# A fourth block product split into seven small ones in the channel product of an attention and mixer kernel

## The chip, the core and the metric

The kernel runs on one core of one Trainium2 chip. The metric is the device time of one execution in microseconds; the kernel before takes 827.31 us (median of three runs, 827.25 to 828.09). The core's engines work side by side and wait for each other by semaphores: TensorE (PE) multiplies matrices into the PSUM buffer, and its weight loads are listed as PEld; VectorE (DVE) and ScalarE (ACT) read PSUM and work on SBUF. Every tensor that the change touches is float32.

## The reference

Routed attention gives `x`, and a mixer follows it. The change lies in the mixer's first channel product, `u @ w_ch1`, and in the relu behind it.

```python
def _moe_ref(x, w_tok1, w_tok2, w_ch1, w_ch2):        # x: (4, 768, 512), from the attention
    xt = x.transpose(0, 2, 1)
    h = np.maximum(xt @ w_tok1, 0.0) @ w_tok2
    u = x + h.transpose(0, 2, 1)
    h2 = np.maximum(u @ w_ch1, 0.0) @ w_ch2           # w_ch1: (512, 1536), w_ch2: (1536, 512)
    return (u + h2).astype(np.float32)
```

## The kernel before

The first channel product is computed transposed, `h2.T = w_ch1.T @ u.T`, as a product of two-by-two blocks with **seven** block products in place of eight (Winograd's form of Strassen's method). The sums of the left blocks (`S1`, `S2`, `S3`, `S4`) are made from weights, those of the right blocks (`T1` to `T4`) from the activations. The table says for each product its PSUM tag, its left and right factor, and the output block to which the running sum in its bank is added when it is done.

```python
SEVEN = {
    "p1":  ("X", "A11", "B11", "c11"),
    "p5":  ("Z", "S1",  "T1",  "c22"),
    "c11": ("Y", "A12", "B21", "c11"),
    "u2":  ("X", "S2",  "T2",  "c12"),    # accumulated on p1, in the same bank
    "c12": ("Z", "S4",  "B22", "c12"),
    "c22": ("X", "S3",  "T3",  "c22"),    # accumulated on p1 + u2
    "c21": ("X", "A22", "T4",  "c21"),
}
```

The rows of the output are worked off in three parts for each of four batches, twelve calls of `ch1_pair` in all. In each call a block product has two chunks (`i`) of 128 rows by 384 columns, and contracts over 256 (`k`), so it takes four matmuls of 384 columns:

```python
def product(psum, a, r, i, start):                    # line 797 of the profile
    c = slice((part + 3 * i) * P, (part + 3 * i + 1) * P)
    for k in range(2):
        nc.tensor.matmul(psum, lhsT=A[a][:, k, c], rhs=R[r][:, k],
                         start=start and k == 0, stop=k == 1, ...)
```

In the first call all seven products are made so. In the other eleven ("with sets") three of them, Y (`c11`), Z (`c12`) and X (`c21`), are themselves two-by-two block products made of seven **small** products, of one matmul of 192 columns each. After every small product the running sum in its bank is added to the output by VectorE, and only then may the next one be accumulated onto that bank:

```python
def set_(psum, which, name, start):                   # line 810 of the profile
    _, a, r, _ = SEVEN[name]
    nc.tensor.matmul(psum, lhsT=left[which][a][:, part * P : part * P + P],
                     rhs=right[which][r], start=start, stop=True, ...)

def set_x(which, tag, name, x):
    if tag: chains[which] = ptile(tag, HS // 2)
    bank = chains[which]
    set_(bank, which, name, name == "p1")
    add(x, both(bank) if len(x.shape) == 3 else bank, x)
```

The head of `ch1_pair` with sets (HS is 384, `n0` and `n1` are the two halves of 192 columns; `between()` works off waiting pieces of other work, such as sums for later; `big` is `product` and then `between()`):

```python
for i in range(2):
    X[i] = ptile("X", HS); big(X[i], "A11", "B11", i, True)
    nc.scalar.copy(out=a11[:, i], in_=X[i])
Z[0] = ptile("Z", HS); big(Z[0], "S1", "T1", 0, True)          # p5, four matmuls over both chunks
nc.scalar.copy(out=p5[:, 0], in_=Z[0])
yc = ptile("X", HS)
set_(yc[:, n0], "Y", "c11", True); set_(yc[:, n1], "Y", "c12", True)
add(a11[:, 0], yc, a11[:, 0])
set_x("Y", "Y", "p1", a11[:, 0, n0])
Z[1] = ptile("Z", HS); big(Z[1], "S1", "T1", 1, True)
nc.scalar.copy(out=p5[:, 1], in_=Z[1])
set_x("Y", None, "u2", a11[:, 0, n1])
set_z("Y", ptile("Y", HS // 2), a11)
big(X[0], "S2", "T2", 0, False); nc.scalar.copy(out=u2[:, 0], in_=X[0])
# ... cut: the second chunk, the rest of Y, Z accumulated on the banks Z[0] and Z[1] ...
relu(a11)                                                      # one instruction, 768 elements
# ... cut: S3 T3, the rest of Z ...
relu(a22)
set_x("Z", None, "c22", c12[:, 1]...)
set_(X[0][:, n0], "X", "c11", False); set_(X[0][:, n1], "X", "c12", False)
nc.scalar.copy(out=a12[:, 0], in_=X[0])
set_(X[1][:, n0], "X", "c21", False)
nc.scalar.copy(out=a12[:, 1], in_=X[1])
set_x("X", "Y", "p1", a12[:, 0, n0]); sum_1()
# ... cut: three more small products of X run inside the second channel product ...
```

Behind each `ch1_pair` follows `ch2_chunks` (line 953 of the profile): the second channel product, 21 chunks of two matmuls of 256 columns, with a VectorE sum into `x` after each. PSUM has eight banks here: three of tag X, three of tag Z and two of tag Y. Between two batches the next batch's activations are turned (`u_steps`) and their right sums made (`u_sums` for the seven products, `set_right_sums` for the small ones).

Of the kernel before, what the change touches and what calls it, by code (L numbers as in the profile page):

```python
# [50 lines left out]
def kernel(  # L51
# [497 lines left out]

    SEVEN = {  # L550
# [16 lines left out]
    def left_weights():  # L567

        w = W["ch1"]
        half = DCH // 2  # L570
        A = pools["A"] = {
            f"A{i + 1}{j + 1}": w[:, 2 * j : 2 * j + 2, half * i : half * i + half]
            for i in range(2)
            for j in range(2)
        }
        extra = pools["wsums"].tile([P, 3, 2, half], F32, name="w1s")
        A["S1"], A["S2"], A["S4"] = (extra[:, i] for i in range(3))
        A["S3"] = A["A21"]
# [22 lines left out]
    def set_lefts():  # L601
        if "l2" not in pools:
            pools["l2"] = pools["w2sums"].tile([P, 3, 3, HS], F32, name="w1ss")
        A, l2 = pools["A"], pools["l2"]
        both = W["ch1"].rearrange("p f (i r c) -> p f i r c", i=2, r=2)[:, 2:4]
        single = A["S4"].rearrange("p f (r c) -> p f r c", r=2)
        for blocks, sums_ in (
            ([both[:, f, :, r] for r in range(2) for f in range(2)], [l2[:, 0:2, m] for m in range(3)]),
            ([single[:, f, r] for r in range(2) for f in range(2)], [l2[:, 2, m] for m in range(3)]),
        ):  # L610
# [9 lines left out]
    def set_rights():  # L620
        uT, t4, r2 = pools["uT"], pools["R"]["T4"], pools["r2"]
        both = uT[:, :, 2:4].rearrange("p n f (k t) -> p n f k t", k=2)
        single = t4.rearrange("p f (k t) -> p f k t", k=2)
        for blocks, sums_ in (
            ([both[:, :, f, k] for f in range(2) for k in range(2)], [r2[:, 0:2, m] for m in range(3)]),
            ([single[:, f, k] for f in range(2) for k in range(2)], [r2[:, 2, m] for m in range(3)]),
        ):
            yield dict(
                zip(("B11", "B12", "B21", "B22", "T1", "T2", "T4", "T3"), blocks + sums_ + blocks[1:2])
            )  # L630

    def set_right_sums():
        pools["r2"] = pools["w2sums"].tile([P, 3, 3, HS // 2], F32, name="uTss")
        for blocks in set_rights():
            yield from winograd_right(blocks)

    def set_blocks():

        (yx, z), (yz, x) = (list(y) for y in (set_lefts(), set_rights()))
        left = {"Y": {k: a[:, 0] for k, a in yx.items()}, "X": {k: a[:, 1] for k, a in yx.items()}, "Z": z}  # L640
        right = {"Y": {k: b[:, 0] for k, b in yz.items()}, "Z": {k: b[:, 1] for k, b in yz.items()}, "X": x}
# [139 lines left out]
    def ch1_pair(part, sets, beside):  # L781
# [6 lines left out]
        p5, u2, c12 = (pools["mlp"].tile([P, 2, HS], F32, name=k) for k in ("p5", "u2", "c12"))  # L788
        A, R = pools["A"], pools["R"]
        left, right = set_blocks() if sets else (None, None)  # L790
        n0, n1 = slice(0, HS // 2), slice(HS // 2, HS)
        X, Y, Z, chains = {}, {}, {}, {}
# [15 lines left out]
        def set_(psum, which, name, start):  # L808
# [6 lines left out]
        def both(psum):  # L815
            return psum.unsqueeze(1).to_broadcast([P, 2, HS // 2])

        def relu(x):
            nc.scalar.activation(out=x, in_=x, func=ACT.Relu)  # L819


        def set_x(which, tag, name, x):
            if tag:
                chains[which] = ptile(tag, HS // 2)
            bank = chains[which]
            set_(bank, which, name, name == "p1")
            add(x, both(bank) if len(x.shape) == 3 else bank, x)

        def set_z(which, bank, x):
            set_(bank, which, "p5", True)  # L830
            add(x[:, :, n1], both(bank), x[:, :, n1])

        a11, a12, a22 = h2["A11"], h2["A12"], h2["A22"]
        for i in range(2):
            X[i] = ptile("X", HS)
            big(X[i], "A11", "B11", i, True)
            nc.scalar.copy(out=a11[:, i], in_=X[i])  # L837
        Z[0] = ptile("Z", HS)
        big(Z[0], "S1", "T1", 0, True)
        nc.scalar.copy(out=p5[:, 0], in_=Z[0])  # L840
        if sets:
            yc = ptile("X", HS)
            set_(yc[:, n0], "Y", "c11", True)
            set_(yc[:, n1], "Y", "c12", True)
            add(a11[:, 0], yc, a11[:, 0])
            set_x("Y", "Y", "p1", a11[:, 0, n0])
        Z[1] = ptile("Z", HS)
        big(Z[1], "S1", "T1", 1, True)
        nc.scalar.copy(out=p5[:, 1], in_=Z[1])
        if sets:  # L850
            set_x("Y", None, "u2", a11[:, 0, n1])
            set_z("Y", ptile("Y", HS // 2), a11)
        else:
            Y[0] = ptile("Y", HS)
            big(Y[0], "A12", "B21", 0, True)
            add(a11[:, 0], Y[0], a11[:, 0])
        big(X[0], "S2", "T2", 0, False)
        nc.scalar.copy(out=u2[:, 0], in_=X[0])
        if sets:
            set_x("Y", None, "c22", a11[:, 1, n1])  # L860
            set_(Z[0][:, n0], "Z", "c11", False)
            set_(Z[0][:, n1], "Z", "c12", False)
        else:
            Y[1] = ptile("Y", HS)
            big(Y[1], "A12", "B21", 1, True)
            add(a11[:, 1], Y[1], a11[:, 1])
        big(X[1], "S2", "T2", 1, False)
        nc.scalar.copy(out=u2[:, 1], in_=X[1])
        if sets:
            set_x("Y", None, "c21", a11[:, 1, n0])  # L870
            relu(a11)
            set_(Z[1][:, n0], "Z", "c21", False)
            add(c12[:, 0], Z[0], u2[:, 0])
            set_x("Z", "Z", "p1", c12[:, 0, n0])
            add(c12[:, 1], Z[1], u2[:, 1])
        else:
            relu(a11)
            big(Z[0], "S4", "B22", 0, False)
            add(c12[:, 0], Z[0], u2[:, 0])
        big(X[0], "S3", "T3", 0, False)  # L880
        add(a22[:, 0], X[0], p5[:, 0])
        if sets:
            set_x("Z", None, "u2", c12[:, 0, n1])
            set_z("Z", ptile("Y", HS // 2), c12)
        else:
            big(Z[1], "S4", "B22", 1, False)
            add(c12[:, 1], Z[1], u2[:, 1])
        big(X[1], "S3", "T3", 1, False)
        add(a22[:, 1], X[1], p5[:, 1])
        relu(a22)  # L890
        if sets:
            set_x("Z", None, "c22", c12[:, 1].rearrange("p (k t) -> p k t", k=2))
            set_(X[0][:, n0], "X", "c11", False)
            set_(X[0][:, n1], "X", "c12", False)
            nc.scalar.copy(out=a12[:, 0], in_=X[0])  # L895
            set_(X[1][:, n0], "X", "c21", False)
            nc.scalar.copy(out=a12[:, 1], in_=X[1])


        def sum_3():  # L900
            nc.vector.scalar_tensor_tensor(
                out=h2["S3"], in0=c12, scalar=0.0, in1=a11, op0=ALU.max, op1=ALU.subtract
            )

        def sum_1():
            nc.vector.scalar_tensor_tensor(
                out=h2["S1"], in0=c12, scalar=0.0, in1=a22, op0=ALU.max, op1=ALU.add
            )

        def sum_4():  # L910
            sub(h2["S4"], a12, h2["S2"])

        if sets:
            set_x("X", "Y", "p1", a12[:, 0, n0])
            sum_1()

            def late_1():
                set_x("X", None, "u2", a12[:, 0, n1])
                set_z("X", ptile("Z", HS // 2), a12)
                sub(h2["S2"], h2["S1"], a11)  # L920

            def late_2():
                set_x("X", None, "c22", a12[:, 1].rearrange("p (k t) -> p k t", k=2))
                relu(a12)
                sum_3()
                sum_4()

            late.extend([late_1, late_2])
        else:
            sum_1()  # L930

            def late_(i):
                product(X[i], "A22", "T4", i, False)
                nc.scalar.activation(out=a12[:, i], in_=X[i], func=ACT.Relu)
                if i == 0:
                    sub(h2["S2"], h2["S1"], a11)
                else:
                    sum_3()
                    sum_4()

            late_(0)
            late.append(lambda: late_(1))
# [210 lines left out]
    for n, b in enumerate(batches):  # L1153
        turning = []
        for part in range(3):
# [9 lines left out]
            if first:  # L1165
                others += list(set_right_sums()) + list(right_weights(1))
# [8 lines left out]
            if part == 2 and not last:  # L1175
                after[3] = lambda: take(turning, len(turning))
                after[15] = lambda: next(usums)
                usums = u_sums()
            ch2_chunks(b, part, last, after)
# [3 lines left out]
            if part == 2 and not last:  # L1183

                steps = list(set_right_sums())
                for m in range(2):
                    steps[m]()
                next(usums)
# [221 lines left out]
```

## Time and profile before

| what | value |
|---|---|
| median time | 827.31 us |
| span of the profiled execution | 825.8 us, granted clock 1.000 |
| busy PE, PEld | 818.2 us (99%), 525.9 us (64%) |
| busy DVE, ACT, POOL | 605.1 us (73%), 381.5 us (46%), 30.7 us (4%) |
| instructions of PE, DVE, ACT | 4282, 1124, 562 |
| the chain that ended last | PE 95%, DVE 4% |

"Busy" is the time in which at least one instruction of the engine ran. A matmul of float32 stands in the trace as two records. Matmuls overlap in the pipeline, and the ends of their records are modelled; so the durations of records are longer than the distance from one start to the next, and it is the starts that tell how fast TensorE goes on. In a line of instruction groups stand the program line, engine, operation, output and input tiles, shapes, count, then busy time and mean duration, and last the idle time before them with what ended it. In a timeline, a line begins with the start and the length in microseconds, and ends, where the engine was idle before, with the idle time and its releaser. A table by stage gives for each stretch its length, then busy time and number of instructions of each engine.

### The profile page before, as it was taken

What the parts mean: (1) busy time and instruction counts of PE and PEld (TensorE: products, weight loads), DVE (VectorE), ACT (ScalarE), POOL (GpSimd) and SP (SyncE); (2) the same over time, 40 slices, a digit from 0 to 9 for tenths busy, and PEclk for the clock granted to TensorE, in tenths of its full rate; (3) what the DMA queues carried; (4) which work ended last, traced back from release to release, by engine and by line L of the source; (5) the groups of instructions that cost most, each with busy time, mean ns of one, the idle gap of its engine ahead of it and who ended that gap; (6) DMA issues with size and microseconds to landing.
All of it is one profiled execution on the core that took longest, in us unless ns stands there. A gap on an engine that the chain in (4) does not pass through costs nothing.

```text
span 825.8 us, 11453 instructions
## 1 busy us (share of the span) xinstructions
PE 818.2 (99%) x4282; PEld 525.9 (64%) x4282; DVE 605.1 (73%) x1124; ACT 381.5 (46%) x562; POOL 30.7 (4%) x28
## 2 busy tenths in 40 slices
PE   8999999999999999999999999999999999999997
PEld 4444444444444444444588787878878788787876
DVE  6879898989898968859776677655667466764645
ACT  5588777787878775136202253121441204521120
POOL 1001010111111000000000000000000000000000
PEclk9999999999999999999999999999999999999999
DMA  8697666767676334143000125000140001400002
GB/s 152 142 159 144 135 142 121 152 143 159 136 156 144 84 96 121 51 156 48 0 1 1 20 39 173 1 0 7 36 113 1 1 1 29 126 1 0 1 2 79
DMA packets 184256, 63.39 MB, mean 77 GB/s; under 512 B 172800, under 2 KB 176896, under 8 KB 183936
## 3 DMA queue, kind: packets, MB, share of 16 engines
q1 hardware_dynamic: 182592, 62.18, 34.5%
q8 instruction: 35, 0.57, 0.3%
q10 hardware_dynamic: 1600, 0.39, 0.2%
q14 instruction: 29, 0.24, 0.1%
HBM read 36.21 MB, written 7.86 MB: 53 GB/s over the span
## 4 chain that ended last, share of the span: by engine, by line
PE 95%; DVE 4%; ACT 0%; issue 0%; ACTq 0%; DVEq 0%
PE sc L413 19%; PE av L455 15%; PE pX L953 14%; PE pX L797 11%; PE pZ L953 7%; PE ph L534 5%; PE pY L810 4%; PE pY L953 4%; PE pZ L797 3%; PE pZ L810 3%; PE pX L771 3%; PE pX L810 2%; PE small L491 2%; PE pZ L771 1%; PE small L304 1%; DVE hA L565 1%
## 5 line engine op out<-in xcount | busy, mean ns | idle before, releaser
L437 ACT ACTIVATE ex<-sc 128x768 f32<-128x768 f32 x192 | 151.0, 812 | 27.2 <-PE sc L413 15.5
L413 PE MATMUL sc<-qkT 64*128 64x384 f32 x768 | 155.3, 483 | 0.0
L445 DVE TENSOR_TENSOR sum<-sum,ex 128x768 f32<-128x768 f32 x128 | 127.8, 998 | 27.6 <-ACT ex L437 15.5
L455 PE MATMUL av<-ex,va 128*64 128x384 f32 x768 | 127.4, 488 | 0.0
L565 DVE TENSOR_TENSOR x<-pX,x 128x256 f32<-128x256 f32 (+1 forms) x168 | 75.9, 458 | 40.9 <-PE pX L953 40.4
L455 PEld LDWEIGHTS av<-ex,va 128*64 128x64 f32 x768 | 53.7, 137 | 71.8 <-issue 67.0
L413 PEld LDWEIGHTS sc<-qkT 64*128 64x128 f32 x768 | 67.8, 187 | 38.3 <-issue 38.0
L837 ACT COPY hA<-pX 128x384 f32<-128x384 f32 x24 | 11.5, 479 | 146.0 <-PE pX L797 146.0
L565 DVE TENSOR_TENSOR hA<-pY,hA 128x192 f32<-128x192 f32 (+1 forms) x90 | 36.7, 408 | 49.9 <-PE pY L810 36.0
L819 ACT ACTIVATE hA<-hA 128x768 f32<-128x768 f32 x35 | 29.5, 843 | 87.1 <-DVE hA L565 87.1
L797 PE MATMUL pX<-uT,wc 128*128 128x384 f32 x192 | 68.0, 487 | 0.0
L413 PE MATMUL sc<-ohT 64*128 64x384 bf16 x384 | 62.5, 323 | 0.0
L797 PEld LDWEIGHTS pX<-uT,wc 128*128 128x128 f32 x192 | 35.7, 190 | 17.6 <-issue 0.6
L462 ACT COPY avrows<-av 128x768 uint16<-128x768 uint16 x32 | 25.5, 798 | 43.9 <-PE av L455 43.9
L565 DVE TENSOR_TENSOR x<-pZ,x 128x256 f32<-128x256 f32 (+1 forms) x84 | 36.4, 455 | 12.0 <-PE pZ L953 11.9
L534 PE MATMUL ph<-x,wt 128*128 128x512 f32 x96 | 41.6, 593 | 0.0
L413 PEld LDWEIGHTS <-ohT 64*128 64x128 bf16 x384 | 18.7, 94 | 33.8 <-issue 9.6
L953 PE MATMUL pX<-wc,hA 128*128 128x256 f32 x144 | 36.9, 380 | 0.4 <-ACT hA L895 0.4
L708 ACT COPY uT<-ucols 128x768 uint16<-128x768 uint16 x32 | 33.3, 1051 | 4.5 <-DMA ucols<-urows 4.5
L953 PE MATMUL pY<-wc,hA 128*128 128x256 f32 x144 | 35.1, 379 | 0.0
L953 PE MATMUL pZ<-wc,hS 128*128 128x256 f32 x144 | 35.0, 379 | 0.0
L797 PE MATMUL pX<-uTs,w1s 128*128 128x384 f32 x96 | 34.9, 486 | 0.0
(178 smaller groups left out, 1266.0 us busy)
## 6 DMA issues: line engine op xcount, KB each, us to landing
raw<-in_moe_w_ch_dram SPq DMA_DIRECT2D x24, 512.0 KB, 4.5
va<-in_v_dram SPq DMA_DIRECT2D x16, 384.0 KB, 3.6
out_dram<-x SPq DMA_DIRECT2D x24, 256.0 KB, 2.5
qk<-in_k_dram SPq DMA_DIRECT2D x60, 96.0 KB, 3.8
qk<-in_q_dram SPq DMA_DIRECT2D x60, 96.0 KB, 3.5
raw<-in_moe_w_tok_dram SPq DMA_DIRECT2D x3, 512.0 KB, 4.2
raw<-in_moe_w_tok_dram SPq DMA_DIRECT2D x4, 384.0 KB, 3.9
spill<-x SPq DMA_DIRECT2D x1, 1536.0 KB, 5.1
```

Of the source, the lines that this page charges most:

```text
L413: nc.tensor.matmul(sc[:, h, 0:HS], lhsT=src[rows, 1, j], rhs=src[rows, 0, HJ * qh : HJ * qh + HJ], start=start, stop=not start,)
L437: nc.scalar.activation(out=ex, in_=sc[:, :, 0:HS], func=ACT.Exp, scale=SM_SCALE)
L445: nc.vector.tensor_tensor(out=acc, in0=acc if j > 1 else st["ex", qh, 0], in1=st["ex", qh, j], op=ALU.add)
L455: nc.tensor.matmul(av[h * D : (h + 1) * D], lhsT=st["va"][:, h, j], rhs=ex[:, h], start=(j == 0), stop=(j == NJ - 1),)
L534: nc.tensor.matmul(pf, lhsT=W["tok1"][:, j, t * P : (t + 1) * P], rhs=xs[b][:, j], start=(j == 0), stop=(j == NJ - 1),)
L565: nc.vector.tensor_tensor(out=dst, in0=a, in1=b, op=ALU.add)
L708: nc.scalar.copy(out=out, in_=pools.pop(("ucols", i)).rearrange("p w j t -> p w (j t)"))
L771: nc.tensor.matmul(psum, lhsT=A[a][:, i], rhs=R[r], start=start, stop=True, skip_group_check=not start,)
L797: nc.tensor.matmul(psum, lhsT=A[a][:, k, c], rhs=R[r][:, k], start=start and k == 0, stop=k == 1, skip_group_check=not start,)
L810: nc.tensor.matmul(psum, lhsT=left[which][a][:, part * P : part * P + P], rhs=right[which][r], start=start, stop=True, skip_group_check=no ...
L819: nc.scalar.activation(out=x, in_=x, func=ACT.Relu)
L953: nc.tensor.matmul(psum, lhsT=h2[a][:, k, i * P : (i + 1) * P], rhs=Bw[w][:, part + 3 * k], start=start and k == 0, stop=k == 1, skip_grou ...
```

## The change

The fourth block product, `p5` (`S1` times `T1`, called P), is made of seven small ones too, in the eleven calls with sets. For that its left sums are made together with those of Z (`pz`, an instruction of twice the width), and its right sums are a new third group (`p`). As all banks are needed for the chains of sums, the order of the products, the banks and the additions is new: the sum `U2` is no longer copied by ScalarE but added to `p5` from its bank, and the relus of `a11` and `a22` are split in two, one for each chunk. The right sums of P for the next batch are made near the end of the second channel product, before those of Y and Z. The call without sets keeps its products, in a function of its own. The aim is to take work off TensorE.

```diff
-            pools["l2"] = pools["w2sums"].tile([P, 3, 3, HS], F32, name="w1ss")
+            pools["l2"] = pools["w2sums"].tile([P, 4, 3, HS], F32, name="w1ss")
...
+        pz = pools["w1s"][:, 0:3:2].rearrange("p i f (r c) -> p i f r c", r=2)
...
+            ([p[:, f, k] for f in range(2) for k in range(2)], [r2[:, 3, m] for m in range(3)]),
...
+        X = [ptile("X", HS), None]
+        big(X[0], "A11", "B11", 0, True)
+        nc.scalar.copy(out=a11[:, 0], in_=X[0])
+        ybe = ptile("Y", HS)
+        direct(ybe, "Y")                                   # two small products
+        add(a11[:, 0], ybe, a11[:, 0])
+        X[1] = ptile("X", HS)
+        big(X[1], "A11", "B11", 1, True)
+        nc.scalar.copy(out=a11[:, 1], in_=X[1])
+        pbe = ptile("Z", HS)
+        direct(pbe, "P")
+        nc.scalar.copy(out=p5[:, 0], in_=pbe)
+        yq, pq = ptile("Y", HS), ptile("Z", HS)
+        chain(yq, "Y", "p1", a11[:, 0, n0])                # one small product, then its sum
+        chain(pq, "P", "p1", p5[:, 0, n0])
         big(X[0], "S2", "T2", 0, False)
+        chain(yq, "Y", "u2", a11[:, 0, n1])
+        yz, pz = ptile("X", HS), ptile("Z", HS)
+        column(yz, "Y", a11)
+        chain(pq, "P", "u2", p5[:, 0, n1])
+        small(pz[:, n0], "P", "p5")
+        nc.scalar.copy(out=p5[:, 1, n1], in_=pz[:, n0])
+        relu(a11[:, 0])
+        add(p5[:, 0, n1], pz[:, n0], p5[:, 0, n1])
+        add(c12[:, 0], X[0], p5[:, 0])                     # before: a copy by ScalarE
         big(X[1], "S2", "T2", 1, False)
+        chain(yq, "Y", "c22", a11[:, 1, n1])
+        chain(pq, "P", "c22", p5[:, 1, n1])
+        direct(ybe, "Z")
+        chain(yq, "Y", "c21", a11[:, 1, n0])
+        small(pq[:, n0], "P", "c21", False)
+        nc.scalar.copy(out=p5[:, 1, n0], in_=pq[:, n0])
+        relu(a11[:, 1])
+        add(c12[:, 0], ybe, c12[:, 0])
+        chain(yz, "Z", "p1", c12[:, 0, n0])
+        add(c12[:, 1], X[1], p5[:, 1])
         big(X[0], "S3", "T3", 0, False)
         add(a22[:, 0], X[0], p5[:, 0])
+        relu(a22[:, 0])
+        chain(yz, "Z", "u2", c12[:, 0, n1])
+        column(pbe, "Z", c12)
         big(X[1], "S3", "T3", 1, False)
         add(a22[:, 1], X[1], p5[:, 1])
+        relu(a22[:, 1])
+        chain(yz, "Z", "c22", c12[:, 1, n1])
+        direct(X[0], "X", False)
+        nc.scalar.copy(out=a12[:, 0], in_=X[0])
+        small(X[1][:, n0], "X", "c21", False)
+        nc.scalar.copy(out=a12[:, 1], in_=X[1])
+        chain(yz, "Z", "c21", c12[:, 1, n0])
+        chain(yq, "X", "p1", a12[:, 0, n0])
+        sum_1()
...
+                after[15] = first_sums                     # T1, and the tile of the small sums
+                after[17] = lambda: (steps[2][0](), steps[2][1]())    # first two right sums of P
```

More of the change, by code (lines that the diff above doesn't have):

```diff
@@ L575, in left_weights @@
         }
-        extra = pools["wsums"].tile([P, 3, 2, half], F32, name="w1s")
+        extra = pools["w1s"] = pools["wsums"].tile([P, 3, 2, half], F32, name="w1s")
         A["S1"], A["S2"], A["S4"] = (extra[:, i] for i in range(3))
@@ L602, in set_lefts @@
         if "l2" not in pools:
-            pools["l2"] = pools["w2sums"].tile([P, 3, 3, HS], F32, name="w1ss")
[L604 to L610, printed above, removed]
+            pools["l2"] = pools["w2sums"].tile([P, 4, 3, HS], F32, name="w1ss")
+        l2 = pools["l2"]
+        yx = W["ch1"].rearrange("p f (i r c) -> p f i r c", i=2, r=2)[:, 2:4]
+        pz = pools["w1s"][:, 0:3:2].rearrange("p i f (r c) -> p f i r c", r=2)
+        for n, both in enumerate((yx, pz)):
+            blocks = [both[:, f, :, r] for r in range(2) for f in range(2)]
+            sums_ = [l2[:, 2 * n : 2 * n + 2, m] for m in range(3)]
             yield dict(
@@ L620, in set_rights @@
     def set_rights():
-        uT, t4, r2 = pools["uT"], pools["R"]["T4"], pools["r2"]
-        both = uT[:, :, 2:4].rearrange("p n f (k t) -> p n f k t", k=2)
-        single = t4.rearrange("p f (k t) -> p f k t", k=2)
+        uT, R, r2 = pools["uT"], pools["R"], pools["r2"]
+        yz = uT[:, :, 2:4].rearrange("p n f (k t) -> p n f k t", k=2)
+        x, p = (R[name].rearrange("p f (k t) -> p f k t", k=2) for name in ("T4", "T1"))
         for blocks, sums_ in (
-            ([both[:, :, f, k] for f in range(2) for k in range(2)], [r2[:, 0:2, m] for m in range(3)]),
-            ([single[:, f, k] for f in range(2) for k in range(2)], [r2[:, 2, m] for m in range(3)]),
+            ([yz[:, :, f, k] for f in range(2) for k in range(2)], [r2[:, 0:2, m] for m in range(3)]),
+            ([x[:, f, k] for f in range(2) for k in range(2)], [r2[:, 2, m] for m in range(3)]),
+            ([p[:, f, k] for f in range(2) for k in range(2)], [r2[:, 3, m] for m in range(3)]),
         ):
@@ L632, in set_right_sums @@
     def set_right_sums():
-        pools["r2"] = pools["w2sums"].tile([P, 3, 3, HS // 2], F32, name="uTss")
-        for blocks in set_rights():
-            yield from winograd_right(blocks)
+        pools["r2"] = pools["w2sums"].tile([P, 4, 3, HS // 2], F32, name="uTss")
+        return [list(winograd_right(blocks)) for blocks in set_rights()]
     def set_blocks():
-        (yx, z), (yz, x) = (list(y) for y in (set_lefts(), set_rights()))
-        left = {"Y": {k: a[:, 0] for k, a in yx.items()}, "X": {k: a[:, 1] for k, a in yx.items()}, "Z": z}
-        right = {"Y": {k: b[:, 0] for k, b in yz.items()}, "Z": {k: b[:, 1] for k, b in yz.items()}, "X": x}
+        (yx, pz), (yz, x, p) = (list(y) for y in (set_lefts(), set_rights()))
+        left = {name: {k: a[:, i] for k, a in two.items()} for two, i, name in
+                ((yx, 0, "Y"), (yx, 1, "X"), (pz, 0, "P"), (pz, 1, "Z"))}
+        right = {"Y": {k: b[:, 0] for k, b in yz.items()}, "Z": {k: b[:, 1] for k, b in yz.items()},
+                 "X": x, "P": p}
         return left, right
@@ L787, in ch1_pair @@
         }
-        p5, u2, c12 = (pools["mlp"].tile([P, 2, HS], F32, name=k) for k in ("p5", "u2", "c12"))
+        p5, c12 = (pools["mlp"].tile([P, 2, HS], F32, name=k) for k in ("p5", "c12"))
         A, R = pools["A"], pools["R"]
-        left, right = set_blocks() if sets else (None, None)
-        n0, n1 = slice(0, HS // 2), slice(HS // 2, HS)
-        X, Y, Z, chains = {}, {}, {}, {}
+        a11, a12, a22 = h2["A11"], h2["A12"], h2["A22"]
         def product(psum, a, r, i, start):
@@ L806, in big, with relu, sum_1, sum_2 @@
                 beside.pop(0)()
-        def set_(psum, which, name, start):
+        def relu(x):
+            nc.scalar.activation(out=x, in_=x, func=ACT.Relu)
+        def sum_1():
+            nc.vector.scalar_tensor_tensor(
+                out=h2["S1"], in0=c12, scalar=0.0, in1=a22, op0=ALU.max, op1=ALU.add
+            )
+        def sum_2():
+            sub(h2["S2"], h2["S1"], a11)
+        def sums_34():
+            nc.vector.scalar_tensor_tensor(
+                out=h2["S3"], in0=c12, scalar=0.0, in1=a11, op0=ALU.max, op1=ALU.subtract
+            )
+            sub(h2["S4"], a12, h2["S2"])
+        (ch1_sets if sets else ch1_plain)(
+            part, product, big, relu, a11, a12, a22, p5, c12, sum_1, sum_2, sums_34
+        )
+    def ch1_plain(part, product, big, relu, a11, a12, a22, p5, c12, sum_1, sum_2, sums_34):
+        X, Z = {}, {}
+        for i in range(2):
+            X[i] = ptile("X", HS)
+            big(X[i], "A11", "B11", i, True)
+            nc.scalar.copy(out=a11[:, i], in_=X[i])
+        for i in range(2):
+            Z[i] = ptile("Z", HS)
+            big(Z[i], "S1", "T1", i, True)
+            nc.scalar.copy(out=p5[:, i], in_=Z[i])
+        for i in range(2):
+            Y = ptile("Y", HS)
+            big(Y, "A12", "B21", i, True)
+            add(a11[:, i], Y, a11[:, i])
+            big(X[i], "S2", "T2", i, False)
+            nc.scalar.copy(out=c12[:, i], in_=X[i])
+        relu(a11)
+        for i in range(2):
+            big(Z[i], "S4", "B22", i, False)
+            add(c12[:, i], Z[i], c12[:, i])
+            big(X[i], "S3", "T3", i, False)
+            add(a22[:, i], X[i], p5[:, i])
+        relu(a22)
+        sum_1()
+        def late_(i):
+            product(X[i], "A22", "T4", i, False)
+            nc.scalar.activation(out=a12[:, i], in_=X[i], func=ACT.Relu)
+            (sums_34 if i else sum_2)()
+        late_(0)
+        late.append(lambda: late_(1))
+    def ch1_sets(part, product, big, relu, a11, a12, a22, p5, c12, sum_1, sum_2, sums_34):
+        left, right = set_blocks()
+        n0, n1 = slice(0, HS // 2), slice(HS // 2, HS)
+        def small(psum, which, name, start=True):
             _, a, r, _ = SEVEN[name]
@@ L813, in set_ @@
             )
[L815 to L856, printed above, removed]
-        big(X[0], "S2", "T2", 0, False)
[L858 to L866, printed above, removed]
@@ L867, in ch1_pair, with direct @@
-        big(X[1], "S2", "T2", 1, False)
[L868 to L879, printed above, removed]
+        def direct(bank, which, start=True):
+            small(bank[:, n0], which, "c11", start)
+            small(bank[:, n1], which, "c12", start)
@@ new lines, in chain, with column @@
+        def chain(q, which, name, x):
+            small(q[:, n0], which, name, name == "p1")
+            src = q[:, n0]
+            if len(x.shape) == 3:
+                src = src.unsqueeze(1).to_broadcast([P, 2, HS // 2])
+            add(x, src, x)
+        def column(z, which, x):
+            small(z[:, n0], which, "p5")
+            add(x[:, :, n1], z[:, n0].unsqueeze(1).to_broadcast([P, 2, HS // 2]), x[:, :, n1])
+        X = [ptile("X", HS), None]
+        big(X[0], "A11", "B11", 0, True)
@@ L880, in ch1_pair @@
+        chain(pq, "P", "c22", p5[:, 1, n1])
[7 more added lines that the diff above has]
+        add(c12[:, 1], X[1], p5[:, 1])
         big(X[0], "S3", "T3", 0, False)
         add(a22[:, 0], X[0], p5[:, 0])
[L882 to L887, printed above, removed]
+        relu(a22[:, 0])
@@ L888, in ch1_pair @@
+        chain(yz, "Z", "u2", c12[:, 0, n1])
+        column(pbe, "Z", c12)
         big(X[1], "S3", "T3", 1, False)
         add(a22[:, 1], X[1], p5[:, 1])
[L890 to L897, printed above, removed]
@@ L900, in sum_3 @@
[L900 to L942, printed above, removed]
@@ new lines, in ch1_sets, with late_1, late_2 @@
+        relu(a22[:, 1])
[6 more added lines that the diff above has]
+        chain(yq, "X", "p1", a12[:, 0, n0])
+        sum_1()
+        def late_1():
+            chain(yq, "X", "u2", a12[:, 0, n1])
+            column(pz, "X", a12)
+            sum_2()
+        def late_2():
+            chain(yq, "X", "c22", a12[:, 1].rearrange("p (k t) -> p k t", k=2))
+            relu(a12)
+            sums_34()
@@ L944, in out_row @@
+        late.extend([late_1, late_2])
     def out_row(b, j):
@@ L1165 @@
             if first:
-                others += list(set_right_sums()) + list(right_weights(1))
+                others += sum(set_right_sums(), []) + list(right_weights(1))
             if n == 0 and part == 1:
@@ L1176, with first_sums @@
                 after[3] = lambda: take(turning, len(turning))
-                after[15] = lambda: next(usums)
                 usums = u_sums()
+                steps = []
+                def first_sums():
+                    next(usums)
+                    steps.extend(set_right_sums())
+                after[15] = first_sums
+                after[17] = lambda: (steps[2][0](), steps[2][1]())
             ch2_chunks(b, part, last, after)
@@ L1183 @@
             if part == 2 and not last:
-                steps = list(set_right_sums())
-                for m in range(2):
-                    steps[m]()
+                yz, x, p = steps
+                yz[0]()
+                yz[1]()
                 next(usums)
                 others += [lambda: next(usums)] * 2
-                others += [lambda m=m: (steps[m](), steps[m + 1]()) for m in (2, 4, 6)]
+                others.append(lambda: [step() for step in (yz[2], p[2], yz[3], p[3])])
+                others += [lambda: None, lambda: (x[0](), x[1]()), lambda: (x[2](), x[3]())]
                 if n == 0:
```

## The prediction, made before the changed kernel was run

> **What bounds the kernel now.** I read the page first, then the chain that ended last, then the table by stage, then one call of `ch1_pair` in the timeline. The page's busy times and the chain's shares:
>
> ```profile
> PE 818.2 (99%) x4282; PEld 525.9 (64%) x4282; DVE 605.1 (73%) x1124; ACT 381.5 (46%) x562; POOL 30.7 (4%) x28
> ...
> PE 95%; DVE 4%; ACT 0%; issue 0%; ACTq 0%; DVEq 0%
> ```
>
> TensorE is nearly never idle and carries the chain. But the busy time is built from modelled ends, so it can hide short waits. I therefore took stretches of the table by stage (length, then busy time and count of PE, PEld, DVE, ACT and POOL): the second product of the first batch's second part, a call of `ch1_pair` right after a change of batch, an ordinary call, and the second product behind that.
>
> ```profile
> 445.95:465.10 19.15, 19.00 (x90) 16.23 (x89) 18.50 (x44) 1.60 (x4) 0.00 (x0) 1.00 0.00 1
> ...
> 501.25:517.80 16.55, 16.44 (x70) 11.85 (x68) 12.38 (x26) 5.07 (x10) 0.00 (x0) 1.00 0.46 170
> ...
> 536.97:553.14 16.17, 16.17 (x70) 11.93 (x69) 6.66 (x15) 4.55 (x9) 0.00 (x0) 1.00 0.00 0
> 553.14:572.31 19.17, 19.17 (x92) 16.82 (x92) 13.01 (x28) 1.60 (x4) 0.00 (x0) 1.00 0.00 1
> ```
>
> The ordinary call lasts 16.17 us, the one after a change of batch 16.55, with nearly twice the VectorE work in it. Now the pace of TensorE inside the ordinary call, from its timeline:
>
> ```profile
> 541.81 1.45 PE L797 MATMUL pZ<-uTs,w1s 128*128 128x384 f32 x4
> ...
> 542.83 0.79 PEld L810 LDWEIGHTS pY<-uTss,w1ss 128*128 128x128 f32 x4 [0.18 <-DVE hA L565]
> 543.10 0.81 PE L810 MATMUL pY<-uTss,w1ss 128*128 128x192 f32 x4
> ...
> 543.75 1.45 PE L797 MATMUL pX<-uTs,w1s 128*128 128x384 f32 x4
> ...
> 545.04 0.49 PE L810 MATMUL pY<-uT,wc 128*128 128x192 f32 x2
> ```
>
> From start to start: four records of 384 columns take 543.10 - 541.81 = 1.29 us, 0.323 each; four of 192 columns take 543.75 - 543.10 = 0.65 us, 0.1625 each. The weight load waited 0.18 us for VectorE, yet the matmuls went on without a gap: the wait was hidden behind the running product. The check: until the second product begins, an ordinary call holds 16 matmuls of 384 columns and 18 small ones, thus 32 and 36 records: 32 x 0.323 + 36 x 0.1625 = 16.19 us, and it lasts 16.17. **Nothing but matmuls is in it**, so every column saved is time saved, as long as no wait comes in.
>
> **What the Trainium skill says.** "Perfetto Trace Analysis", section Identifying the Most-Contended Engine: busy time of matmuls is no good measure of how close a kernel is to its limit. Agreed: the records above last 1.45 us where the pace is 1.29; hence I count starts. "TensorE: Matmul & The Clock Gate", section "Wait — 56ns, not 53.3ns?": a warm matmul costs its columns plus a fixed 2.5 ns or so. The trace agrees on the fixed part: 2 x 162.5 - 323 = 2 ns, so cutting a product into half-width matmuls costs TensorE nothing to speak of. "VectorE: DVE Perf Modes", section The TRN2 errata: a float32 `tensor_tensor` takes (N + 151) / 0.96 ns, so small pieces pay a fixed part each time. That gives 357, 557 and 957 ns for 192, 384 and 768 elements; the trace has 356, 552 to 558 and about 950. "PSUM — Partial Sum Buffer", section The four PSUM rules: a partial sum may be read, synchronised, amid an accumulation group. The chains of small products live on that, and no run of before shows that it has a cost of its own.
>
> **The change on TensorE.** P before: two chunks by two matmuls of 384 columns, 8 records, 8 x 0.323 = 2.584 us. P after: seven small matmuls, 14 records, 14 x 0.1625 = 2.275 us. Saved 0.309 us a call, in 11 calls **3.4 us**. Records: 14 - 8 = 6 more a call, 66 in all. This lies wholly on the path.
>
> **The change on VectorE.** Sums of 192 columns a call: new are P's `p1`, `u2`, `c22` and the sum of its column; Z's last broadcast sum of 384 becomes two of 192; and `c12` gets one more sum of 384, which before was a ScalarE copy. By the durations: 4 x 0.356 + (2 x 0.356 - 0.55) + 0.55 = 2.14 us a call, 23.5 us over 11. Beside that, P's right sums, 4 of 192 for each of 4 batches: 16 x 0.35 = 5.6 us; and Z's left sums of 128 elements (0.28 us) become 256 wide (0.415 us), 12 x 0.135 = 1.6 us. Together 31 us more of VectorE, about 636 us. In an ordinary call it goes from 6.66 to 8.8 of 16 us: beside other work, if each sum is in time.
>
> **The change on ScalarE.** Before, a call has eight copies of 384 (0.479 us) and three relus of 768 (0.843): 6.36 us, part of it in the second product. After, five such copies, two of 192 (some 0.31 each, an estimate: 0.479 less 192 x 0.86 ns, the slope given below), four half relus (0.51, estimate below) and one whole: 5.9 us. Slightly less, and of no weight, for ScalarE is busy 4.55 of 16.17 us in the call.
>
> **Are the sums in time?** I laid the new order out by hand with the pace above and the latencies of the trace: VectorE starts 0.20 us after a matmul's slot ends (550.22 + 4 x 0.323 = 551.51, sum at 551.71), a sum of 192 lasts 0.36. A chain's next step can thus go 0.6 to 0.65 us after the step before, if VectorE is free. Time that the new order puts between: Y `p1` to Y `u2` one small and one big, 0.33 + 1.29 us; `u2` to `c22` three small and one big, 2.3 us; Y `c22` to `c21` three small, 0.98 us; P `c22` to `c21` the same; Z `c22` to `c21` three small, 0.98 us. In the worst of these VectorE has one more sum of 0.28 us pitch before it, so some 0.1 to 0.3 us stay. The last gate: the second product's first matmul takes bank X[0], which ScalarE must have copied. From the end of the last S3 product: sum 0.20 + 0.56, half relu 0.51 (estimate: 0.843 less 384 x 0.86 ns, the slope between 0.482 us for 384 and 0.812 for 768 elements), copy 0.46, all in all 1.7 us; six small products lie between, 1.96 us. So it holds with 0.2 us. **An ordinary call should last 16.17 - 0.31 = 15.86 us.**
>
> **At a change of batch** before, TensorE waits 16.55 - 16.17 = 0.38 us for the first sum of Y, which stands behind seven wide sums. After, VectorE does T2, T3, T4 and the first sums of Y and Z in the first 4.6 us, then Y's `p1`; the next Y product comes at 5.84 us, with a whole microsecond to spare. The later four right sums fit before `c22`, at 8.4 us. So the 0.38 us go, three times: **1.1 us**. The last call's extra 0.56 us (16.73 us by the table by stage) I leave: there TensorE waits for the copy of X[0], a wait that stays.
>
> **New waits** I expect in the first batch: VectorE is busy 18.50 of 19.15 us in its second part, where the trace has about 0.4 us of waits, and gets some 0.5 us more there, 1.4 us in the part before. I give 0.6 us back for that and for small misses.
>
> Sum: 827.31 - 3.4 - 1.1 + 0.6 = **823.4 us**, 0.5% less.
>
> **Rivals.** (a) *VectorE or a chain of sums becomes the bound.* For it: 31 us more work, in pieces, on chains that TensorE has to wait for; tight gaps of 0.98 us; the full stretch in the first batch. Against it: VectorE would still be idle nearly half of an ordinary call. If one chain slipped by 0.3 us in each call, the 3.4 us would be gone and the time 826 to 827; if two did, 829 to 830. (b) *The weight loads bind.* A load record lasts 190 ns, over the 162.5 ns pace of small matmuls, and there are more of them. Against it: in the ordinary call ten small records run in a row from 551.51 to 553.14 at 0.163. If loads bound, it would show there. Gain then as computed or less, 824 to 825. (c) *A bank waits.* All eight banks are held to the end, and the second product now takes X[0] at once, where before an early free bank (that of Y's first two products) was at hand. If the 0.2 us are not there, 0.1 to 0.2 us a call are lost: 825 to 826. (d) *Better than computed*: the first batch's present 0.4 us and the last call's 0.56 go too: 822.5.
>
> **Range and chances.** The saving has a hard ceiling: 3.4 + 1.1 + 0.4 + 0.56 = 5.5 us, so not under 821.8. Most of the weight lies at full or nearly full saving, a tail on (a) and (c): 822.3 to 825.8. Two per cent are 16.5 us; neither the saving nor any wait above comes near it, so within 2% is all but sure.
>
> **What would show it.** In the changed profile: 66 more PE records (4348); ordinary calls of 15.86 us, calls after a change of batch nearly as short; DVE busy near 636 us; second products of 19.17 us unchanged. The prediction fails if ordinary calls hold idle gaps on TensorE released by VectorE (a) or ScalarE (c), if small records come slower than 0.163 us (b), or if the first batch's second products stretch by over a microsecond.

## The result, and the profile after

The changed kernel takes **823.12 us** (median of six runs, 822.92 to 823.68), the kernel before in the same comparison 827.46 us. The ratio is 0.9948, with a 95% interval from 0.9935 to 0.9961: 4.3 us, half a per cent, faster. The prediction was 823.4 us.

The same parts of the page for the changed kernel, engines first and then the chain that ended last:

```profile
PE 814.2 (99%) x4348; PEld 535.5 (65%) x4348; DVE 631.1 (77%) x1206; ACT 374.7 (46%) x573; POOL 30.7 (4%) x28
...
PE 98%; DVE 1%; issue 0%; ACT 0%; DVEq 0%; ACTq 0%
```

TensorE has the 66 records more that were computed, and is busy 4.0 us less. VectorE got 26 us more, and its share of the chain fell from 4% to 1%. Now the table by stage (length, then busy time and count of PE, PEld, DVE, ACT and POOL), for the stretches that answer to those shown of before: the second product of the first batch's second part, the call after a change of batch, an ordinary call, and the second product behind it.

```profile
445.62:465.33 19.71, 19.57 (x93) 16.66 (x92) 19.43 (x45) 0.95 (x2) 0.00 (x0) 1.00 0.00 1
...
500.41:516.58 16.17, 16.13 (x75) 12.65 (x74) 14.02 (x34) 4.64 (x11) 0.00 (x0) 1.00 0.41 150
...
535.69:551.56 15.87, 15.87 (x76) 12.69 (x75) 8.45 (x21) 4.61 (x11) 0.00 (x0) 1.00 0.00 1
551.56:570.66 19.10, 19.10 (x92) 16.92 (x91) 13.28 (x29) 0.95 (x2) 0.00 (x0) 1.00 0.01 1
```

The first of these lines must not be set against the 19.15 us of the prediction's table. That table ended the stretch of before at 465.10, while the next call's first matmul starts at 465.81. The whole stretch of before, and the weight load in it that TensorE waits for, are these:

```profile
445.95:465.81 19.86, 19.71 (x94) 16.55 (x92) 18.80 (x45) 1.60 (x4) 0.00 (x0) 1.00 0.00 1
...
458.59 2.46 PEld L953 LDWEIGHTS pX<-wc,hS 128*128 128x128 f32 x12 [0.55 <-DVE x L565]
```

The same load after the change:

```profile
458.11 2.46 PEld L966 LDWEIGHTS pX<-wc,hS 128*128 128x128 f32 x12 [0.54 <-DVE x L566]
```

So this stretch did not grow from 19.15 to 19.71 us; it fell from 19.86 to 19.71.

The ordinary call fell from 16.17 to 15.87 us, though VectorE works 8.45 us in it and not 6.66. The second product fell from 19.17 to 19.10. The call after a change of batch fell from 16.55 to 16.17, so it is still 0.30 us over an ordinary one. In the timeline of that call one sees why; the lines are those around the second S3 product:

```profile
513.89 0.56 DVE L566 TENSOR_TENSOR c<-pZ,c 128x384 f32<-128x384 f32 x1
...
514.36 0.35 DVE L563 TENSOR_TENSOR uTs<-uTs 128x192 f32<-128x192 f32 x1
...
514.63 0.35 DVE L563 TENSOR_TENSOR uTss<-uTs,uTss 128x192 f32<-128x192 f32 x1
...
514.90 0.55 DVE L566 TENSOR_TENSOR hA<-pX,p 128x384 f32<-128x384 f32 x1
...
515.50 0.30 PEld L871 LDWEIGHTS pX<-uTss,wc 128*128 128x128 f32 x2 [0.34 <-DVE hA L566]
515.50 0.59 PE L871 MATMUL pX<-uTss,wc 128*128 128x192 f32 x2
```

VectorE works through its queue without a gap. The sum that frees bank X[1] (`hA<-pX,p`) could start at about 514.5, but stands behind the last two right sums of X (`uTs`, `uTss`) and starts at 514.90. The small product X `c21` goes onto that bank, and waits until 515.50. It also reads the last of X's right sums, but that was done at 514.63 + 0.35 = 514.98; the sum that frees the bank ends at 514.90 + 0.55 = 515.45, so it is the bank that X `c21` waits for. Before, TensorE waited in these calls for the first sum of Y; that wait is gone, and this one has come.

### The profile page after: what moved, and what is told of

Same layout as the page of the kernel before. It is cut to its first block, busy times and chain, and to the rows that moved or that the text cites. A ratio compares the mean times of both kernels' runs of the same rounds, so it can differ in the third digit from the quotient of the medians.

```text
span 821.6 us, 11693 instructions
## 1 busy us (share of the span) xinstructions
PE 814.2 (99%) x4348; PEld 535.5 (65%) x4348; DVE 631.1 (77%) x1206; ACT 374.7 (46%) x573; POOL 30.7 (4%) x28
## 4 chain that ended last, share of the span: by engine, by line
PE 98%; DVE 1%; issue 0%; ACT 0%; DVEq 0%; ACTq 0%
PE sc L413 19%; PE av L455 15%; PE pX L966 15%; PE pX L798 12%; PE pZ L966 7%; PE ph L534 5%; PE pY L871 5%; PE pZ L871 4%; PE pX L871 4%; PE pY L966 4%; PE pX L774 3%; PE small L491 2%; PE pZ L774 1%; PE small L304 1%; PE pZ L798 1%; PE pY L774 1%
## 5 line engine op out<-in xcount | busy, mean ns | idle before, releaser
L810 ACT ACTIVATE hA<-hA 128x384 f32<-128x384 f32 (+1 forms) x57 | 34.0, 597 | 85.4 <-DVE hA L566 85.1
L798 PE MATMUL pX<-uT,wc 128*128 128x384 f32 x192 | 69.8, 487 | 0.0
L894 ACT COPY hA<-pX 128x384 f32<-128x384 f32 x11 | 5.3, 479 | 131.3 <-PE pX L798 131.3
```

What stands on the lines that cost most here:

```text
L798: nc.tensor.matmul(psum, lhsT=A[a][:, k, c], rhs=R[r][:, k], start=start and k == 0, stop=k == 1, skip_group_check=not start,)
```

## The experiments

The first four runs ask where the gain comes from, and what the new wait hangs on.

**P as four large matmuls, in the new order.** P's products and sums become those of before, and P's small sums on VectorE are not made:

```diff
-        direct(pbe, "P")
+        product(pbe, "S1", "T1", 0, True)
...
-        chain(pq, "P", "p1", p5[:, 0, n0])
...
-        chain(pq, "P", "u2", p5[:, 0, n1])
-        small(pz[:, n0], "P", "p5")
-        nc.scalar.copy(out=p5[:, 1, n1], in_=pz[:, n0])
+        product(pq, "S1", "T1", 1, True)
+        nc.scalar.copy(out=p5[:, 1], in_=pq)
```

> The order, the banks and the half relus of the changed kernel, but P (S1 T1) again as four matmuls of 384 columns; P's small sums on VectorE are not made. Theory (the gain is the columns that TensorE no longer streams): each call with sets gets back 8 x 0.323 - 14 x 0.1625 = 0.31 us, so ordinary calls of 16.17 to 16.19 us and about 823.1 + 3.4 = 826.5 us; with less VectorE work the waits after a change of batch may go, 0.3 us each, so 825.6 to 826.5. Rival (the gain comes from the new order, the split relus and waits that went): ordinary calls stay near 15.87 us and the time at 823 to 824.

Measured: 828.03 us, ratio to the kernel before 1.0008 (0.9999 to 1.0016). The whole gain is gone, and the time is 1.5 us above the most that I expected. A call after a change of batch, and an ordinary call:

```profile
501.20:518.07 16.87, 16.54 (x69) 11.79 (x68) 12.49 (x28) 4.48 (x10) 0.00 (x0) 1.00 0.41 151
537.18:553.44 16.26, 16.26 (x69) 11.82 (x68) 6.95 (x17) 4.54 (x10) 0.00 (x0) 1.00 0.00 0
```

The ordinary call has 0.39 us more than in the changed kernel: the 0.30 of the columns, and 0.09 more at Y's last product, which now follows Y `c22` too closely. P's small products had filled that time. After a change of batch, X `c21` even waits 0.6 us behind the same two right sums of X, with *less* work for VectorE. So the new order, with its split relus, is worth nothing without P's small products: the columns are the gain, and the small products also serve as cover for each other's chains.

**Whole relus in the changed kernel.**

```diff
-        relu(a11[:, 0])
...
-        relu(a11[:, 1])
+        relu(a11)
...
-        relu(a22[:, 0])
...
-        relu(a22[:, 1])
+        relu(a22)
```

> The changed kernel with the relus of a11 and of a22 each as one instruction of 768 elements again, at the place of the later half. Theory (the halves are there to free bank X[0] in time): the copy of X[0] stands behind the second relu of a22 and comes 0.843 - 0.522 = 0.32 us later; in the changed kernel it ends 0.26 us before the second product's first matmul and its weights load is due 0.10 us after it, so TensorE waits 0.15 to 0.25 us in each of 11 calls, ended by the copy on ScalarE: 824.8 to 825.9 us. Rival (the relus are off the path): ordinary calls stay at 15.87 us and the time at 823.1.

Measured: 825.72 us, ratio 0.9979 (0.9971 to 0.9986), so 2.6 us of the gain go. The timeline at the end of an ordinary call:

```profile
550.96 0.84 ACT L810 ACTIVATE hA<-hA 128x768 f32<-128x768 f32 x1 [3.08 <-DVE hA L566]
...
551.71 0.46 ACT L936 COPY hA<-pX 128x384 f32<-128x384 f32 x1
...
552.23 0.73 PEld L964 LDWEIGHTS pX<-wc,hA 128*128 128x128 f32 x4 [0.24 <-ACT hA L936]
```

The copy that frees X[0] ends at 551.71 + 0.46 = 552.17, and the weights load behind it starts at 552.23. By the starts of the matmuls this costs 0.2 us in each of six calls with their second products. In the three calls after a change of batch it costs 0.45 us, with a VectorE sum named as the last releaser; why it is more there is not shown. The first call with sets and the last lose nothing on balance. Together that is the 2.6 us. In the changed kernel the same copy is early enough:

```profile
550.40 0.52 ACT L810 ACTIVATE hA<-hA 128x384 f32<-128x384 f32 x1 [1.42 <-DVE hA L566]
...
550.83 0.46 ACT L938 COPY hA<-pX 128x384 f32<-128x384 f32 x1
...
551.39 0.79 PEld L966 LDWEIGHTS pX<-wc,hA 128*128 128x128 f32 x4
```

It ends at 551.29, 0.10 us before the load and 0.26 before the matmul at 551.55. The half relus are no ornament: they pay for the tight use of the banks.

**The kernel before, with half relus alone** (`relu(a11)` and `relu(a22)` each in two, in the calls with sets).

> The kernel before, with nothing of the change but the relus of a11 and a22 in two halves in the eleven calls with sets. Theory (columns): ordinary calls stay at 16.17 us, as nothing but matmuls is in them; the wait of 0.06 us at the first late sum of X in the second product goes, since the copy of X[0] comes 0.32 us earlier, so 0 to 0.7 us faster: 826.8 to 827.4. Rival (the relus held up the kernel before): 2 us or more faster, under 825.5.

Measured: 826.87 us, ratio 0.9993 (0.9985 to 1.0002): not to be told from the kernel before by its time. The trace shows where something small lies:

```profile
536.57:552.74 16.17, 16.17 (x69) 11.92 (x68) 6.66 (x15) 5.06 (x12) 0.00 (x0) 1.00 0.00 0
552.74:571.85 19.11, 19.11 (x93) 16.93 (x92) 13.04 (x28) 1.28 (x3) 0.00 (x0) 1.00 0.01 2
```

The call stays at 16.17, and the second product is at 19.11 as in the changed kernel. The 0.06 us there come from the earlier copy of X[0], which lets the first late sum of X in on time.

**P's last two right sums made earlier**, within the second product ahead of a change of batch:

```diff
                 after[17] = lambda: (steps[2][0](), steps[2][1]())
+                after[18] = lambda: steps[2][2]()
+                after[19] = lambda: steps[2][3]()
...
-                others.append(lambda: [step() for step in (yz[2], p[2], yz[3], p[3])])
+                others.append(lambda: [step() for step in (yz[2], yz[3])])
```

One of these sums overwrites a block of T1 that T2, made later, still reads. So this kernel computes other values than the reference and serves for its times alone; the number and kind of its instructions are those of the changed kernel.

> The changed kernel with the last two right sums of P made after the next two chunks of the second product too, before the change of batch, where VectorE idles 0.3 to 0.4 us after most chunks. Theory (the new wait of 0.3 us after a change of batch comes from VectorE's queue: the last sum from bank X[1] stands behind delayed sums, so the product X c21 waits for that bank): 0.55 us less work in that queue, the calls after a change of batch go from 16.17 or 16.31 to 15.9 us, 0.9 us in all: 822.2 us. Rival (the wait is for the last right sums of X themselves, or the tail of the second product pays for it): no gain, 823.0 to 823.5.

Measured: 822.98 us, ratio 0.9946 (0.9932 to 0.9959), and all three calls after a change of batch take 16.17 us. The wait at X `c21` is there as before; only a further 0.1 us at Y `c21`, in one call, went. My theory of a queue late from the head of the call on fell: VectorE idles 0.62 us at Y `c21` and has caught up by then. What remained was the rival, the right sums of X themselves.

**X's right sums at another place.** One more point at which waiting work is taken up:

```diff
         chain(pq, "P", "c22", p5[:, 1, n1])
+        between()
```

> The changed kernel with one more point in the call at which waiting work is taken up, behind P's c22: after a change of batch the first two right sums of X go there, into a stretch where VectorE idles 0.62 us for the product Y c21, and the last two follow behind the first S3 product, in place of the second. Theory (the wait at X c21 is the order of VectorE's queue around S3: x2 and x3 stand right ahead of the sum that frees bank X[1]): the 0.3 us wait goes in each of the three calls after a change of batch; these take 15.9 to 16.0 us, the whole 822.2 to 822.5 us. Rival (VectorE's queue is late as a whole from the head of the call on): the wait stays at 0.2 to 0.3 us or moves to Y c21, 823.1 us.

Measured: 822.19 us, ratio 0.9935 (0.9921 to 0.9948). The same call after a change of batch, and an ordinary one:

```profile
500.17:516.04 15.87, 15.87 (x76) 12.69 (x74) 14.07 (x34) 4.70 (x11) 0.00 (x0) 1.00 0.40 153
535.14:551.00 15.86, 15.86 (x75) 12.68 (x74) 8.44 (x21) 4.59 (x11) 0.00 (x0) 1.00 0.00 1
```

Both are the same length, with the same 14 us of VectorE work in the first as in the changed kernel. Not the amount of work but its place in the queue made the wait. (One of the three calls keeps 0.14 us, at Y `c21`.)

**The loading of the counts at another place.** `both = fits_load()`, which stands between the last call and its second product, moved to the start of the second batch.

> The changed kernel with the loading of the three counts into registers, which stands between the last call and its second product, moved to the start of the second batch. Theory now (the 0.49 us before the last second product are this loading, on TensorE's instruction stream, and not the copy of X[0] that the trace names): the last call takes 15.9 in place of 16.36 us, and the loading costs as much or nothing at its new place, 822.6 to 823.2 us. The prediction's reading (a wait for the copy of X[0], which stays): the last call stays at 16.36 us.

Measured: 822.92 us, ratio 0.9944 (0.9930 to 0.9957). In the changed kernel the trace names a copy by ScalarE as the releaser of the wait behind the last call. That is the first line; the second is the last call of this run in the table by stage.

```profile
797.56 0.73 PEld L966 LDWEIGHTS pX<-wc,hA 128*128 128x128 f32 x4 [0.60 <-ACT hA L940]
```

```profile
781.36:797.23 15.87, 15.87 (x76) 12.68 (x74) 8.45 (x21) 4.61 (x11) 0.00 (x0) 1.00 0.00 0
```

The last call is an ordinary one now. It was the loading that TensorE waited for, not the copy, whatever releaser stood last in the trace. At its new place, in a call with a backlog on VectorE, it costs 0.2 us.

**The first batch's weight sums later**: `others += [lambda: None] * 5` ahead of the sums for the third part.

> The changed kernel with the weight sums for the third part put off by five chunks in the second part's second product of the first batch. Theory (the 0.4 us in this stretch are VectorE falling behind, when the seven products' sums and the weight sums come at once): spread out, the waits of 0.3 and 0.1 us at S3's first chunks go, 19.7 to 19.3 us, the whole 822.7 us. Rival (VectorE is simply full there, 19.43 of 19.71 us): the waits move to a later chunk or to the next call, 823.1 us.

Measured: 823.05 us, ratio 0.9943 (0.9930 to 0.9957); the difference from the changed kernel lies within the spread. The trace shows the stretch itself:

```profile
445.94:465.25 19.31, 19.31 (x93) 16.82 (x92) 18.85 (x44) 0.95 (x2) 0.00 (x0) 1.00 0.00 1
```

It is 0.4 us shorter than 19.71, and the next call does not lose it again: it takes 15.97 us in both kernels, though one of the weight sums now falls into it. VectorE is busy nearly all the stretch, and TensorE no longer waits for it.

**More VectorE work in every call**: three sums of 384 elements, their results unused.

```diff
         add(c12[:, 0], X[0], p5[:, 0])
+        extra()
...
         add(c12[:, 1], X[1], p5[:, 1])
+        extra()
...
         relu(a22[:, 0])
+        extra()
```

> The changed kernel with three more VectorE sums of 384 elements (0.47 us of its queue each, results unused) in each of the 11 calls: behind the two sums into c12 that free a bank or start a chunk, and behind the first a22. Theory (in an ordinary call VectorE has room): ordinary calls stay within 0.1 us of 15.87, with about 10 us of VectorE in them; the calls after a change of batch, where its queue is full, lose 0.5 to 1.4 us; 824.5 to 828 us. Rival (a, VectorE is all but the bound now): every call gets longer by most of 1.4 us, 835 us and more.

Measured: 827.09 us, ratio 0.9996 (0.9988 to 1.0004). Call after a change of batch, and ordinary call:

```profile
500.43:517.80 17.37, 16.66 (x75) 12.54 (x74) 15.41 (x37) 4.64 (x11) 0.00 (x0) 1.00 0.38 140
536.91:552.82 15.91, 15.91 (x76) 12.65 (x74) 9.52 (x24) 4.55 (x11) 0.00 (x0) 1.00 0.00 1
```

An ordinary call takes 1.4 us of VectorE's queue for 0.04 us of time; the three calls after a change of batch pay 1.1 to 1.2 us each, nearly the whole of it. Rival (a) is false in the ordinary calls. In these three, work added to VectorE's queue costs nearly its full length, though the run with X's sums at another place shows that the work which the change itself brings fits there.

**All three repairs, and the changed kernel again on the same chip.** The loading of the counts stands here ahead of the second batch's second call.

> The changed kernel with all three repairs: the extra point for the right sums of X, the weight sums of the third part put off by five chunks, and the loading of the counts moved to the head of the second batch's second call, where VectorE has no backlog (in the run with the loading at the start of the second batch it cost 0.2 us there). Theory: the gains are in different stretches and add up, 0.8 (calls after a change of batch) + 0.4 (first batch) + 0.55 us (last call) = 1.7 us under the changed kernel, 821.4 us; all ordinary calls 15.87 us, none of the 11 over 16.02. Rival (waits removed in one place come back in the next): 822 us or more.

> The changed kernel itself once more, as the measure for the run with the three repairs on the same chip. Both theories expect 823.1 us and ordinary calls of 15.87 us.

Measured: **821.28 us** (ratio 0.9918, 0.9904 to 0.9931) against 823.27 us for the changed kernel (0.9942, 0.9929 to 0.9956). All calls with sets take 15.86 to 16.00 us, the last one included. This version is 2.0 us under the changed kernel, and the waits that were removed did not come back.

## Why the prediction was right, and where it was not

The time fell within 0.3 us of the prediction, and its main step held to a few hundredths of a microsecond. But two of its smaller terms were wrong, and a third was missing. That they cancelled was luck.

- **TensorE's columns: right.** 0.31 us a call was computed, 0.30 measured (16.17 to 15.87), 3.3 us in all. That a call holds nothing but matmuls, before and after, carried this. With P in four large matmuls the gain is gone.
- **VectorE's work: right in kind.** 31 us were computed, the profile has 26. The durations of all VectorE instructions, added up one by one in the two traces, rose by 30.4 us (647.7 to 678.1), as computed. But sums that follow each other at once overlap, and busy time counts the overlap once: at the change of batch the two right sums and the sum behind them start at 514.36, 514.63 and 514.90, 0.27 us apart, where each right sum lasts 0.35.
- **The last gate, bank X[0]: right.** Expected was 0.2 us of room; the copy ends 0.26 us before the matmul. The half relu, estimated at 0.51 us, takes 0.522 to 0.527.
- **"At a change of batch ... the 0.38 us go, three times": wrong.** The first sum of Y is in time, as laid out; the next Y product comes at 506.23 - 500.41 = 5.82 us, without a wait. But I followed the right sums of X only as work to be fitted in, and not as what stands ahead of the sum that frees bank X[1]. The calls take 16.17, 16.31 and 16.17 us, where 16.55 less the 0.30 of the columns would be 16.25 with the old wait whole. So of the 1.1 us next to nothing came: 0.07 us each in two calls, and 0.07 lost in the third, which also waits at Y `c21`. Moving X's sums showed the cause: the first and the third of these calls then take 15.87 us, the second 16.01.
- **"New waits in the first batch", 0.6 us: they did not come.** By the starts of the matmuls the stretch has waits of 0.30 and 0.10 us, and before, cut at its true end, it had 0.31 and 0.10. VectorE's work in it rose by 0.63 us (18.80 to 19.43) and did no harm. That putting the weight sums off by five chunks removes the waits says that the time at which these sums come made them, not their amount.
- **Missing: the second product.** The prediction held these unchanged at 19.17 us. Most are 0.06 us shorter, since the copy of X[0] now precedes the first late sum of X; that is 0.7 us over all, with 0.14 in the first batch's second part. The kernel before with half relus alone shows the same 19.11 us. As the "hard ceiling" of 5.5 us left this term out, it was none: with all three repairs the span is 819.5 us, 6.3 under that of before.
- **"The last call's extra 0.56 us ... TensorE waits for the copy of X[0]": the reason was wrong**, the amount nearly right (0.49 us stayed). It is the loading of the counts, as its move showed.

So the sum reads 3.3 (columns) + 0.1 (changes of batch) + 0.7 (second products) + 0.1 (last call) = 4.2 us, which is the difference of the two profiled spans (825.8 and 821.6). The formula of the Trainium skill ("VectorE: DVE Perf Modes", section The TRN2 errata) gives the length of a single sum rightly, 357 ns for 192 elements where the trace has 0.35 to 0.36 us. But in a queue in which sums overlap, such lengths cannot be added up; there the distance of the starts counts, 0.27 us.

## What to carry to other kernels

Where a stage's length equals the sum of its matmuls' start-to-start times, a saved column is saved time, and the hand layout has only to prove that no wait comes in. For that, follow for every bank *which instruction frees it and what stands ahead of that instruction in its engine's queue*; the amount of free time of the engine says little. Small instructions on a busy engine are also cover for the chains around them: with P in four large matmuls an ordinary call lost 0.09 us more than its columns. And a table by stage is only as good as its cuts: set each cut at the first matmul of the next stage, or a wait drops out of one row and into another.

## What the runs showed of the hardware that was not expected

A 192-column float32 record keeps its 0.1625 us pace though each weight load's record lasts 0.19 us; even the longer rows of small products after the change hold it (six such products, 12 records, take 551.55 - 549.60 = 1.95 us at the end of an ordinary call). So the prediction's rival (b), that the weight loads bind, is out. Loading three counts into registers between two stages held TensorE for about 0.5 us, and the trace put the wait down to a copy that had ended 0.35 us earlier (796.73 + 0.48 = 797.21, and the load began at 797.56). It cost 0.2 us in a call with a full VectorE queue, and nothing visible in an ordinary call.
